# Gated scan with routed experts: the third early job in two 16-bit halves in place of plain fp32

## The chip, the core and the metric

One core of one Trainium2 chip. The metric is the device time of one execution in microseconds. Three runs of the kernel before gave 760.76, 761.78 and 762.32 us; their median, 761.78, is the time before.

## What is computed

The first half is a gated scan along the sequence, the second a mixture of experts with one expert per token (the softmax weights are cut here to what matters):

```python
f = lower + (1 - lower) / (1 + exp(-f_logit))         # (4, 3648, 256)
for t in range(S): h = f[:, t] * h + (1 - f[:, t]) * x[:, t]; y[:, t] = h
tok = y.reshape(14592, 256)
g = argmax(tok @ w_group); e = argmax(tok @ w_expert[g])   # 4 groups of 4 experts
out = g_w * e_w * (maximum(tok @ w1[g, e], 0) @ w2[g, e])  # 256 -> 1024 -> 256
```

## The kernel before, in words

The tokens are scanned in 29 units of 512 (lines 500 to 618). For a unit, its two inputs are loaded (`p1_load`, L180), ScalarE makes the gate (`p1_tanh`, `p1_affine`, L218 and L228), VectorE multiplies and scans (`p1_tb`, `p1_gate`, L244, L255, L265), TensorE transposes the result into rows and makes the routing logits (L283, L302, L315), ScalarE copies them (L285, L307, L316), and VectorE finds each token's expert and its place in that expert's list (L329 to L433; the place is `posi`, L433). GpSimd then writes the rows into the lists in DRAM with indirect DMAs, the scatters (L392). Units 0 to 7 are routed one by one, then two by two.

The experts' work is cut into jobs. Sixteen early jobs (kind "A", `EARLY`) start while the scan goes on: each takes the last rows of a list that has filled far enough by a given unit, and an expert chosen by `choose` (L648), which SP reads back as a value. Jobs 0 to 3 have 256 rows each; job 0 is cut at unit 4, job 1 at 6, jobs 2 and 3 at 8. Sixteen late jobs (kind "B") take the rest of the lists after the scan.

A job's weights come in four pieces of 128 by 1024 (`job_weights`, L933). In a split job, a piece lands in one of eight `st` buffers, which the inputs of units 4 to 7 use first; ScalarE casts it to fp16 (L949) and VectorE takes the rest in bf16 (L951). The rows are loaded (L924), transposed (L1007) and split in the same way (`xh` L1016, `xl` L1017), and the places and weights of the rows are copied aside (`meta`, L1022). The first stage (`m1_step`, L1046) takes three 16-bit products (L1063 to L1065) for each of 8 column blocks and 2 halves of K, then ScalarE's Relu (`hh`, L1068) and VectorE's remainder (`hl`, L1069), four times for 256 rows. The second stage (`m2_step`, L1080) takes three products again (L1095) for 8 blocks and each 128 rows; ScalarE scales the result (L1107), GpSimd scatters it to the output (L1109).

A job with index below `RAW` is plain ("raw"): its weights go straight into their own buffers (L937), its rows are copied (L1013) and nothing is split. The first stage (`raw1`, L1033) has one fp32 product where a split job has three, and a Relu (L1044); the second (`raw2`, L1072, L1076) likewise.

The order. SP's instructions run in the order in which the program is written. On TensorE, VectorE and ScalarE it is fixed by hand only up to the first job's preparation (L1232); after that a planner, which estimates the time of each instruction, lays down each engine's order, and the engines run that order whatever the chip's times are. `issue_after` keeps an instruction behind another in the plan: by `BEHIND` (L44, L950), a job's splits on VectorE stand behind the places of a unit; 7 is the eighth unit. The scan's work is written between the steps of the jobs (`bg_step`, L1219), at a rate that meets each job's due mark. A job's preparation (`prep_thunks`, L1174) is written while the job before it is multiplied; it also fetches further pieces of weights: up to 4 ahead for a raw job, up to 8 for a split one (L1181). A split job's second stage is written behind the next first stage, a raw job's directly behind its own:

```python
for pj, pc in ([pending] if pending else []) + ([(j, ch)] if j.raw else []):
    for t in range(len(pj.parts[pc])):
        m2_step(pj, pc, t)
pending = None if j.raw else (j, ch)
```

Of the kernel before, what the change touches and what calls it, by code (L numbers as in the profile page):

```python
# [32 lines left out]
ROWS_AT = {4: 5, 6: 7}  # L33
USED = float(1 << 22)
STG_BUFS = 8
RAW = 3
XR_BUFS = 6
ROW_BUFS = 6
O_BUFS = 5
# [1 line left out]
AHEAD = 3  # L41
STAGED = range(4, 8)
BEGIN = 6
BEHIND = {2: 7, 3: 7}  # L44
MT = -(-max(CAPS) // 128)
QUARTERS = (13, 14, 15)
ZX_SP = 12
# [5 lines left out]
def gated_scan_moe(ctx: ExitStack, tc, zx, lower, wroute, wexp, out, S):  # L53
# [28 lines left out]
    def bank(tag):  # L82
        return ps.tile([P, UNIT], F32, name=f"ps_{tag}", tag=tag, bufs=PS_BUFS[tag])
# [361 lines left out]
    def p1_thunks(us, groups, parts):  # L445
# [42 lines left out]
        def routing(v):  # L488
            grp = ends[v]
            T = sum(unit_range(x)[1] - unit_range(x)[0] for x in grp) // P  # L490
            G = {}

            def bind(G=G, first=grp[0]):
                G.update(cur.pop("G"))

            def bound(G=G, first=grp[0]):
                G["rows"] = group_rows.pop(first)
            return bind, bound, route_thunks(G, T, True)

        for u in us + [us[-1] + 1]:  # L500
            seq = []
            if u <= FAST:
# [12 lines left out]
                if ending:  # L515
                    bind, bound, (s1, f4x, s2, f3, f4, s6, f5, s7s) = routing(u - 1)
                    if u - 1 == BEHIND[2]:
                        f4.mark = "ranked"
# [302 lines left out]
    def make_job(kind, idx):  # L821
# [6 lines left out]
        while at < j.len:  # L828
# [13 lines left out]
            at += w  # L842
        j.raw = kind == "A" and idx < RAW
        j.wh, j.wl, j.st = {}, {}, {}
# [99 lines left out]
    def job_split(j, i):  # L944
# [4 lines left out]
        nc.scalar.copy(j.wh[i], j.st[i])  # L949
        with tc.issue_after(placed[BEHIND[j.idx] * 4]) if j.kind == "A" and j.idx in BEHIND else ExitStack():  # L950
            nc.vector.tensor_tensor(out=j.wl[i], in0=j.st[i], in1=j.wh[i], op=ALU.subtract)  # L951

    def job_xt(j, pi):
# [49 lines left out]
        tp = bank("p")  # L1003
        with tc.issue_after(ranked[BEHIND[2]]) if j.raw and j.idx == 1 else ExitStack():
            for k in range(KD):
# [74 lines left out]
    def m2_step(j, ch, t, pm=None):  # L1080
# [7 lines left out]
        if j.raw:  # L1088
            u = BEHIND[2] if j.idx == 0 else -1
            with tc.issue_after(ranked[u]) if u in ranked else ExitStack():  # L1090
# [238 lines left out]
```

## Time and profile before

| | |
|---|---|
| median of three runs | 761.78 us |
| the profiled execution | 760.23 us |
| its span, first to last instruction | 758.4 us |
| TensorE products (PE), busy | 718.3 us, 95% |
| TensorE weight loads (PEld), busy | 638.5 us, 84% |
| VectorE (DVE), busy | 531.1 us, 70% |
| ScalarE (ACT), busy | 450.3 us, 59% |
| GpSimd (POOL), busy | 296.0 us, 39% |

The profile is one execution on the chip. Busy time is the time in which an engine had an instruction under way; products overlap in TensorE's pipeline, so the sum of single durations is more than the busy time. In a timeline, a row gives the start, the duration, the engine, the line, the operation and its shapes; in brackets stands how long the engine was idle before, and what ended the wait. The chain is followed back from the last instruction: each step to what released it, or to the instruction before it on its engine.

### The profile page before, as it was taken

The numbers are of one execution on the slowest core, as the hardware profiler recorded it, in microseconds if no ns is written. First come the engines' busy times: TensorE is split into PE (matmuls) and PEld (weight loads), VectorE is DVE, ScalarE is ACT, GpSimd is POOL, SyncE is SP. The second block draws the span as 40 slices with busy tenths as digits, with TensorE's granted clock in tenths as the row PEclk, the third lists the DMA queues.
The fourth block names the chain that finished last, engine by engine and source line by source line (L and its number), as shares of the span: only waits on it lengthen the run. The fifth ranks groups of instructions, "written<-read, shape, count | busy, mean of one in ns | idle before, by whom it ended". The sixth has DMA issues, their size and how long they took to land.

```text
span 758.4 us, 21398 instructions
## 1 busy us (share of the span) xinstructions
PE 718.3 (95%) x8115; PEld 638.5 (84%) x8115; DVE 531.1 (70%) x1155; ACT 450.3 (59%) x824; POOL 296.0 (39%) x273
## 2 busy tenths in 40 slices
PE   3669999999999999999999999999999999999995
PEld 1557888888888888898899899999899999999995
DVE  6998779999999985687455735463754675557652
ACT  6667778876886864445454534453544465556552
POOL 3656355566855663631122212222222222223223
PEclk9969999999999999999999999999999999999998
DMA  8988899998897854567885752424354455566521
GB/s 326 397 276 278 249 378 336 382 298 294 300 315 248 251 177 149 131 178 181 187 201 155 161 129 77 133 83 122 120 143 107 142 164 139 159 177 196 172 70 35
DMA packets 101384, 152.01 MB, mean 200 GB/s; under 512 B 60898, under 2 KB 70913, under 8 KB 98464
## 3 DMA queue, kind: packets, MB, share of 16 engines
q1 hardware_dynamic: 86752, 103.27, 47.3%
q0 software_dynamic: 11408, 30.02, 10.8%
q10 hardware_dynamic: 3120, 17.34, 6.8%
q8 instruction: 64, 1.05, 0.6%
q14 instruction: 40, 0.33, 0.2%
HBM read 112.66 MB, written 38.40 MB: 199 GB/s over the span
## 4 chain that ended last, share of the span: by engine, by line
PE 62%; DVE 19%; DMA 8%; issue 4%; ACT 3%; SPq 1%; POOL 1%; POOLq 0%; ACTq 0%; DVEq 0%
PE ps_m L1095 30%; PE ps_m L1063 6%; PE ps_m L1065 6%; PE ps_m L1064 6%; DVE h L255 4%; DVE w L951 4%; PE ps_p L1063 3%; DMA st<-in_wexp_dram 3%; PE ps_p L1065 3%; PE ps_p L1064 3%; DVE hl L1069 3%; DMA xs<-rows,posi 3%; PE ps_p L283 1%; DVE zt L244 1%; ACT w L949 1%
## 5 line engine op out<-in xcount | busy, mean ns | idle before, releaser
L1095 PE MATMUL ps_m<-w,hh 128*128 128x256 bf16 (+7 forms) x2480 | 304.2, 251 | 0.0
L1095 PE MATMUL ps_m<-w,hl 128*128 128x256 f16 (+3 forms) x1240 | 250.3, 251 | 0.0
L1095 PEld LDWEIGHTS <-hh 128*128 128x128 f16 (+4 forms) x2480 | 183.1, 99 | 21.2 <-issue 2.7
L1063 PE MATMUL ps_m<-xh,w 128*128 128x256 f16 (+10 forms) x782 | 187.4, 254 | 4.7 <-DVE hl L1069 4.7
L1065 PE MATMUL ps_m<-xh,w 128*128 128x256 f16 (+10 forms) x782 | 187.2, 254 | 0.0
L1064 PE MATMUL ps_m<-xl,w 128*128 128x256 bf16 (+10 forms) x782 | 187.2, 254 | 0.0
L392 POOL DMA_INDIRECT xs<-rows,posi x114 | 141.1, 1238 | 111.3 <-ACT rows L287 25.6
L951 DVE TENSOR_TENSOR w<-st,w 128x1024 bf16<-128x1024 f32 x116 | 140.1, 1219 | 52.8 <-ACT w L949 52.5
L1109 POOL DMA_INDIRECT out_dram<-o,info x71 | 83.7, 1179 | 233.2 <-ACT o L1107 203.1
L1069 DVE SCALAR_TENSOR_TENSOR hl<-ps_m,hh 128x512 bf16<-128x512 f32 (+9 forms) x166 | 109.7, 666 | 57.2 <-ACT hh L1068 56.9
L1068 ACT ACTIVATE hh<-ps_m 128x512 f16<-128x512 f32 (+9 forms) x166 | 97.4, 588 | 65.3 <-PE ps_m L1065 64.9
L949 ACT CAST w<-st 128x1024 f16<-128x1024 f32 x116 | 120.4, 1050 | 14.1 <-PE ps_m L1095 8.1
L1064 PEld LDWEIGHTS <-w 128*128 128x128 f16 x1088 | 106.5, 98 | 12.4 <-issue 5.4
L1063 PEld LDWEIGHTS <-w 128*128 128x128 f16 x1088 | 106.5, 98 | 8.4 <-issue 1.2
L1065 PEld LDWEIGHTS <-w 128*128 128x128 bf16 x1088 | 106.4, 98 | 7.1 <-issue 0.2
L1095 PEld LDWEIGHTS <-hl 128*128 128x128 bf16 (+3 forms) x1240 | 97.7, 99 | 10.1 <-issue 0.7
L1109 POOL DMA_INDIRECT out_dram<-o,meta x51 | 59.9, 1175 | 104.8 <-ACT o L1107 93.7
L1107 ACT ACTIVATE o<-ps_m,info 128x256 f32<-128x256 f32 (+4 forms) x71 | 31.6, 445 | 73.6 <-PE ps_m L1095 65.8
L1069 DVE SCALAR_TENSOR_TENSOR hl<-ps_p,hh 128x512 bf16<-128x512 f32 (+13 forms) x65 | 41.9, 644 | 42.4 <-ACT hh L1068 42.1
L1063 PE MATMUL ps_p<-xh,w 128*128 128x256 f16 (+17 forms) x306 | 71.5, 249 | 0.0
L1064 PE MATMUL ps_p<-xl,w 128*128 128x256 bf16 (+17 forms) x306 | 71.5, 249 | 0.0
L1065 PE MATMUL ps_p<-xh,w 128*128 128x256 f16 (+17 forms) x306 | 71.5, 249 | 0.0
(179 smaller groups left out, 821.1 us busy)
## 6 DMA issues: line engine op xcount, KB each, us to landing
st<-in_wexp_dram SPq DMA_DIRECT2D x116, 512.0 KB, 7.6
zt<-in_zx_dram ACTq DMA_DIRECT2D x16, 1024.0 KB, 7.4
xs<-blank SPq DMA_DIRECT2D x28, 258.0 KB, 8.0
zt<-in_zx_dram SPq DMA_DIRECT2D x6, 1024.0 KB
w<-in_wexp_dram SPq DMA_DIRECT2D x12, 512.0 KB, 9.6
st<-in_zx_dram SPq DMA_DIRECT2D x8, 512.0 KB, 13.6
xr<-xs SPq DMA_DIRECT2D x14, 258.0 KB, 3.2
xs<-rows,posi POOLq DMA_INDIRECT x114
```

Source lines behind the costliest of these rows:

```text
L255: sn = nc.vector.tensor_tensor_scan(out=h[:, k, c0 - a:c1 - a], data0=ff[:, k, c0 - a:c1 - a], data1=uu[:, k, c0 - a:c1 - a], initial=init ...
L392: sc = nc.gpsimd.indirect_dma_start(out=xs_v[G["t0"] + t][:, :], out_offset=bass.IndirectOffsetOnAxis(ap=R["posi"][:, t:t + 1], axis=0), i ...
L949: nc.scalar.copy(j.wh[i], j.st[i])
L951: nc.vector.tensor_tensor(out=j.wl[i], in0=j.st[i], in1=j.wh[i], op=ALU.subtract)
L1063: nc.tensor.matmul(po, w1_at(j.wh, k, c), xh[:, k], start=(k == 0), stop=False)
L1064: nc.tensor.matmul(po, w1_at(j.wh, k, c), xl[:, k], start=False, stop=False)
L1065: nc.tensor.matmul(po, w1_at(j.wl, k, c), xh[:, k], start=False, stop=(k == KD - 1))
L1068: eviction[0] = nc.scalar.activation(hi, pv, AF.Relu).ins
L1069: nc.vector.scalar_tensor_tensor(out=j.hl[ch][:, cs[0]:cs[-1] + 1, 0:w], in0=pv, scalar=0.0, in1=hi, op0=ALU.max, op1=ALU.subtract)
L1095: nc.tensor.matmul(pm[i * q:i * q + n, 0:dw], h[ch][:, c, ts], w2_at(w, c)[:, i * dw:(i + 1) * dw], start=(c == 0 and s == 0), stop=(c == ...
L1107: nc.scalar.activation(o[s, 0:dw], pm[s, 0:dw], AF.Copy, scale=lt.bitcast(F32)[s, r, 1:2])
L1109: nc.gpsimd.indirect_dma_start(out=out_v[out_n[0]].rearrange("n (g d) -> (n g) d", g=g), out_offset=bass.IndirectOffsetOnAxis(ap=lt[s, r, ...
```

## The change

The constants `RAW` and `BEHIND` are changed, and nothing else. Job 2 is no longer raw: it takes the code of the split jobs, with its splits on VectorE behind the eighth unit's places. Jobs 0 and 1 stay raw. Job 3's splits are no longer kept behind these places. `BEHIND[2]`, which three other lines use for the eighth unit, keeps its value.

```diff
-RAW = 3
+RAW = 2
...
-BEHIND = {2: 7, 3: 7}
+BEHIND = {2: 7}
```

## Rows read from the trace of the kernel before

**Rows 1.** Busy us (count) by stretch: PE, PEld, DVE, ACT, POOL; clock, DMA share, GB/s.

```profile
80.00:130.00 50.00, 49.45 (x394) 41.08 (x394) 39.43 (x89) 39.54 (x77) 23.57 (x20) 1.00 0.96 327
130.00:270.00 140.00, 134.87 (x1430) 118.13 (x1428) 137.35 (x300) 110.46 (x210) 89.68 (x69) 1.00 0.87 293
270.00:720.00 450.00, 449.75 (x5345) 409.81 (x5343) 271.56 (x538) 233.84 (x402) 126.23 (x113) 1.00 0.56 149
```

**Rows 2.** The chain that ended last, 130 to 270 us, its shares by line.

```profile
by line: DVE w L951 15.3%; DVE h L255 13.2%; DVE hl L1069 11.8%; issue 7.4%; PE ps_m L1095 7.4%; DMA st<-in_wexp_dram 6.9%; DVE zt L244 5.3%; DMA xs<-rows,posi 4.4%; DVE xl L1017 3.8%; ACT w L949 2.7%; PE ps_m L1063 2.0%; PE ps_m L1065 1.6%
```

**Rows 3.** Timeline of TensorE, the third job's first products.

```profile
99.09 0.59 PE L1041 MATMUL ps_m<-xh,w 128*128 128x256 f32 x2
```

**Rows 4.** Pieces of the chain that ended last: start, us, what.

```profile
76.32 2.59 PE ps_m L1076 x12
79.35 1.73 PE ps_m L1041 x8
...
282.81 5.24 PE ps_m L1095 x48
```

**Rows 5.** Lines by source, whole span: count, then ns min/median/max.

```profile
L951 DVE TENSOR_TENSOR w<-st,w x116: 1184/1220/1227, 101.7 to 739.9; 128x1024 bf16<-128x1024 f32 x116
L1017 DVE TENSOR_TENSOR xl<-ps_p,xh x21: 415/678/692, 111.3 to 305.2; 128x512 bf16<-128x512 f32 x15, 128x256 bf16<-128x256 f32 x6
L1022 DVE COPY meta<-xr x21: 152/157/365, 111.9 to 305.8; 128x4 int32<-128x4 int32 x15, 128x2 int32<-128x2 int32 x6
L1069 DVE SCALAR_TENSOR_TENSOR hl<-ps_m,hh x166: 425/682/693, 120.4 to 743.3; 128x512 bf16<-128x512 f32 x139, 128x480 bf16<-128x480 f32 x3, 128x440 bf16<-128x440 f32 x2, 128x416 bf16<-128x416 f32 x2
L949 ACT CAST w<-st x116: 1032/1045/1117, 100.6 to 738.8; 128x1024 f16<-128x1024 f32 x116
L1016 ACT CAST xh<-ps_p x21: 364/586/684, 110.1 to 304.1; 128x512 f16<-128x512 f32 x15, 128x256 f16<-128x256 f32 x6
L1013 ACT COPY xh<-ps_p x3: 355/367/373, 57.2 to 88.0; 128x256 f32<-128x256 f32 x3
```

**Rows 6.** Timeline of VectorE, 80 to 102 us: the four longest waits.

```profile
83.96 0.32 DVE L329 TENSOR_REDUCE mx<-Lg 128x40 f32<-128x160 f32 x1 [3.31 <-ACT Lg L316]
...
92.70 1.23 DVE L244 SCALAR_TENSOR_TENSOR zt<-zt 128x1024 f32<-128x1024 f32 x1 [1.20 <-ACT zt L228]
...
96.52 0.32 DVE L329 TENSOR_REDUCE mx<-Lg 128x40 f32<-128x160 f32 x1 [1.27 <-ACT Lg L316]
...
101.67 1.23 DVE L951 TENSOR_TENSOR w<-st,w 128x1024 bf16<-128x1024 f32 x1 [2.03 <-ACT w L949]
```

**Rows 7.** SP's timeline, and the landing times of the plain jobs' weights.

```profile
64.75 2.09 SPq L937 DMA_DIRECT2D w<-in_wexp_dram  x4
...
DMA to landing us min/median/max: 8.9/9.6/13.4
```

**Rows 8.** Timeline of ScalarE, its longest waits from 76 to 100 us.

```profile
80.29 0.47 ACT L1107 ACTIVATE o<-ps_m,xr 128x256 f32<-128x256 f32 x1 [3.14 <-DMA w<-in_wexp_dram]
...
99.29 0.47 ACT L1107 ACTIVATE o<-ps_m,xr 128x256 f32<-128x256 f32 x1 [2.80 <-PE ps_m L1076]
```

**Rows 9.** Timeline of VectorE, the eighth unit's places.

```profile
68.88 0.22 DVE L433 TENSOR_REDUCE posi<-sc 128x4 int32<-128x64 f32 x1
```

**Rows 10.** A scatter's landing in the chain that ended last.

```profile
109.52 7.04 DMA xs<-rows,posi
```

**Rows 11.** Timeline of VectorE and GpSimd, a split and the scatter beside it.

```profile
104.82 1.20 DVE L951 TENSOR_TENSOR w<-st,w 128x1024 bf16<-128x1024 f32 x1
...
105.24 1.63 POOL L392 DMA_INDIRECT xs<-rows,posi  x1 [4.23 <-ACT rs L307]
...
107.17 0.97 POOL L392 DMA_INDIRECT xs<-rows,posi  x1 [0.30 <-issue]
```

**Rows 12.** Timeline of VectorE, the end of job 3's splits and its xl.

```profile
107.80 2.33 DVE L951 TENSOR_TENSOR w<-st,w 128x1024 bf16<-128x1024 f32 x2
...
111.34 0.66 DVE L1017 TENSOR_TENSOR xl<-ps_p,xh 128x512 bf16<-128x512 f32 x1
```

## The prediction

> **What bounds the kernel now.** I read the busy time by stretch first, because the shares of the whole span average over stages with different limits. Three stretches matter. From 80 to 130 us TensorE is busy 49.45 of 50 us, while VectorE has 10.57 us idle and ScalarE 10.46. From 130 to 270 TensorE (134.87 of 140) and VectorE (137.35) are both nearly full, VectorE a little more: 98.1%. From 270 to 720 TensorE alone is full [rows 1]. Then I read the chain that ended last. Between 130 and 270 its largest lines are VectorE's: the weight splits of L951, the scans of L255, the halves of L1069; TensorE's L1095 has 7.4% of it [rows 2]. So the scan stage ends when VectorE is through, and behind it TensorE runs without a gap to the end. A shift of VectorE's work before 270 us reaches the end nearly whole; a saving of TensorE before 130 us reaches it only if VectorE also gets there sooner.
>
> The edit lies where these regimes meet: the third job (index 2) starts its first stage at 99.09 us [rows 3].
>
> **Part 1, TensorE.** A plain fp32 product appears as two instructions: 12 of them stand 2.59 us in the chain, 8 stand 1.73 us, so 0.216 us for one and 0.432 for a product. Three 16-bit products cost 5.24/48 = 0.109 each, 0.327 in place of 0.432 [rows 4]. The job has 16 first-stage products (8 column blocks by 2 halves of K) and 16 second-stage ones (2 parts by 8). Removed: 32 x 0.432 = 13.8 us; added: 96 x 0.109 = 10.5. TensorE saves **3.3 us**.
>
> **Part 2, VectorE.** Added: four splits of 1.220, one xl of 0.678, one meta copy of 0.157, four hl of 0.682 [rows 5]: 4.88 + 0.68 + 0.16 + 2.73 = **8.45 us**. Nothing is taken off it. Its cover is the idle time of 80 to 130 us, of which four waits are large: 3.31 (until 83.96), 1.20, 1.27 and 2.03 (until 101.67) [rows 6]. The first three, 5.78 us, lie ahead of the job's first product, and the splits with xl and meta (5.72) would have to use them. Two splits fit into the 3.31; the next two fill 1.20 and 1.27; xl and meta, 0.84, find nothing. The four hl come after 101 us, when the gap of 2.03 is nearly over; I give them 0.6 of it and 1.0 of the small gaps behind, so 1.1 of 2.73 is uncovered. Uncovered in all: 0.84 + 1.1, about **2.0 us**. Bounds: everything covered gives 0, nothing covered 8.45. I take the value near the low end, because the large gaps and the work are of about one size.
>
> **Part 3, ScalarE.** Added: four casts of 1.045 and one xh cast of 0.586; removed: two copies of 0.367 [rows 5]. Net +4.0 us; the four Relu evictions per job stay. The weights are issued from 64.75 on and land 8.9 to 13.4 us later [rows 7], so between 74 and 80; ScalarE waits 3.14 us until 80.29 and 2.80 until 99.29 [rows 8]. These two gaps, 5.94 us, are the cover, and I price the casts at nothing. If the first gap is lost, because the casts stand in program order ahead of a landing, scans and logits behind them are late: up to 13.4 - 9.6 = 3.8 us, an end of the range.
>
> **Part 4, the holds.** The job's VectorE splits are placed behind the eighth unit's places. That unit's positions are done at 69.1 us [rows 9], the weights land after 74, so the hold costs no time; it only keeps the planner from putting a split earlier in VectorE's order. Job 3's hold goes: its splits now wait for their casts anyway (2.03 until 101.67 [rows 6]), so zero, unless the planner moves one ahead of a scan; then one such wait, 2.03 us, is the price above, and the gain below is at most the same.
>
> **Part 5, queues and buffers.** SP's four loads of the job keep their place (piece order is unchanged) but go into `st` buffers, those of units 4 and 5, freed long before 64.75: zero. Job 4 then takes job 2's buffers instead of those of units 6 and 7, so its loads wait for job 2's splits, and, since a split job prefetches further, three of these loads stand on SP ahead of the later choice of a job. If the splits are done by 97 us this hides behind job 3's four casts; if not, what is late is job 4's weights and, through SP, the next rows. The chain there runs through a scatter's landing, 7.04 us from 109.52 on [rows 10], and the row load behind it; SP is free again by then, so zero, and at worst one split, 1.22. POOL: the job's two output scatters lose their wait behind the list scatters; they reach nobody else before the end.
>
> **Part 6, the scatters.** A POOL scatter takes 0.97 us alone; the one at 105.24 met a split that ran from 104.82 to 106.02 and took 1.63 [rows 11]: 0.66 us later. The added splits lie where the lists' scatters are issued, and the chain passes through one of these at 109.52 [rows 10]. I count zero, since the added splits are done before that one, and 0.66 in the range.
>
> [...]
>
> **Sum.** TensorE's 3.3 us lie ahead of a stretch that VectorE sets, so they turn into idle time: counted 0. VectorE's uncovered work: +2.0. The profiled execution took 760.23 us (span 758.4 and 1.83 around it), so 762.2 for such a one; that execution stands 1.55 below the median of 761.78, so the median goes to **763.8**. A measurement of this kernel can tell about 0.2%, 1.5 us, from no change, so this is just on the slower side.
>
> **Rivals.**
> Faster, TensorE sets the pace: in 80 to 130 it is the full engine [rows 1], and the gaps of VectorE there end with ScalarE, which waited on TensorE. If the gaps take all 8.45 us and the stage behind starts as much earlier as TensorE does, the 3.3 us arrive whole: 761.78 - 3.3 = **758.5**. Against it: the chain of 130 to 270 is VectorE's. Chance 0.25.
>
> No difference: VectorE fills 80 to 130 as well as it fills 130 to 270, 98.1%, leaving 0.95 us idle, so up to 9.6 of the 10.57 are used; 8.45 - 9.6 = -1.2 at best, about 0 with one gap missed: 760.6 to 763.3. Chance 0.27.
>
> Clearly slower, a wait on TensorE's in-order queue: a plain job's second stage directly follows its first, while a split job's is issued behind the next job's first stage. If the planner puts job 3's first products ahead of job 2's second stage, TensorE stands from about 107 (99.1 and some 8 us for 5.2 us of products among the scan stage's) until job 3's last split (110.1) and its xl (112.0) [rows 12] with 5.2 us of ready work queued behind. That is 3 to 5 us on top of the 2.0: **767 to 769**. It decides only if nothing of the scan stage fills the hole. Chance 0.12. The forecast itself (+1.5 to +4) has 0.36.
>
> That the change doesn't do what it says can only be so for the hold, which binds nothing in time (part 4).
>
> **The numbers.** Slower: 0.36 + 0.12 = 0.48; within 0.2%: 0.27; faster: 0.25. The range runs from the faster rival, 758.5, to the wait rival with its upper price, 768.5; each side leaves out under a tenth. The forecast's own range is 763.3 to 766.
>
> **What would show it.** Right: TensorE's busy time to 130 us falls by about 3 us and its idle time between 130 and 270 rises from 5.1 towards 8 us; VectorE's gaps of 3.31, 1.20 and 1.27 are filled with L951; its idle time between 80 and 130 falls below 4 us; the last scan ends about 2 us later. Wrong: the scan stage ends earlier than before (TensorE set the pace), or a new wait of TensorE on hl, xl or L951 between 105 and 115 (the queue rival), or a new ScalarE wait on the weights' landing before 80 us.

## The result and the profile after

The changed kernel takes **771.29 us** (median of six runs, 767.36 to 772.42), the kernel before 762.25 in six runs beside it: a ratio of **1.0105** (95% interval 1.0087 to 1.0124). The direction was forecast, the size was not: +2.0 us were predicted, about four times that came, and 771.29 lies above the range. The profiled execution of the changed kernel took 772.17 us (span 770.4), 11.9 more than that of before; the median shift is 9.0, and 1.05% of 762 is 8.0. Rows of one execution are read below with that in mind.

First the busy line of the page and the first two stretches of [rows 1] in the changed kernel (PE, PEld, DVE, ACT, POOL; granted clock, DMA share, GB/s).

```profile
PE 721.4 (94%) x8147; PEld 640.1 (83%) x8147; DVE 537.9 (70%) x1165; ACT 453.9 (59%) x827; POOL 294.5 (38%) x273
```

```profile
80.00:130.00 50.00, 43.36 (x343) 33.68 (x342) 38.74 (x83) 33.74 (x65) 18.89 (x16) 0.93 0.84 278
130.00:270.00 140.00, 136.00 (x1443) 120.56 (x1441) 138.53 (x303) 113.55 (x214) 88.56 (x69) 0.99 0.91 302
```

The loss arises between 80 and 130 us: TensorE is busy 43.36 us instead of 49.45, at a mean granted clock of 0.93 instead of 1.00, and ScalarE does 5.8 us less there although it was given more to do. VectorE, which got 8.45 us of new work, is idle for 11.26 us instead of 10.57. All three wait for something. From 130 to 270 TensorE runs a little fuller than before (136.00 against 134.87). The lower clock of this stretch belongs to this execution: in another one of the same kernel (`a_again2` below, as slow against its kernel before) the clock stays at 1.00 there, and TensorE is busy even less:

```profile
80.00:130.00 50.00, 41.47 (x353) 32.96 (x352) 39.90 (x85) 35.04 (x67) 20.15 (x16) 1.00 0.83 283
```

The chain that ended last shows the same from its other side. Between 130 and 270 us its largest lines are now TensorE's, where [rows 2] had VectorE's:

```profile
by line: PE ps_m L1095 30.0%; PE ps_m L1063 10.9%; PE ps_m L1064 10.4%; PE ps_m L1065 10.3%; PE ps_p L283 6.4%; DMA zt<-in_zx_dram 5.3%; PE ps_p L302 3.7%; DVE w L951 3.5%; DVE h L255 3.5%; issue 3.1%; PE ps_p L1007 2.9%; ACT w L949 2.4%; D
```

TensorE's holes before 140 us have become work that it must catch up, with nothing left to hide them.

**Where it waits.** ScalarE's timeline around the job, in the changed kernel (start, duration, engine, line, operation, tiles; in brackets the idle time before it and what released it):

```profile
84.28 0.33 ACTq L204 DMA_DIRECT2D zt<-in_zx_dram  x1
84.67 0.60 ACT L1044 ACTIVATE hh<-ps_m 128x512 f32<-128x512 f32 x1 [4.59 <-DMA xr<-xs]
...
97.28 0.34 ACTq L204 DMA_DIRECT2D zt<-in_zx_dram  x1
97.66 1.06 ACT L218 ACTIVATE zt<-zt 128x1024 f32<-128x1024 f32 x1 [4.31 <-DMA xs<-blank]
...
107.31 1.06 ACT L218 ACTIVATE zt<-zt 128x1024 f32<-128x1024 f32 x1 [4.55 <-DMA zt<-in_zx_dram]
```

The same two transfers in the kernel before, on the same engine:

```profile
79.85 0.33 ACTq L204 DMA_DIRECT2D zt<-in_zx_dram  x1
...
87.16 0.33 ACTq L204 DMA_DIRECT2D zt<-in_zx_dram  x1
```

How to read it: an eviction from PSUM (L1044) has no use for a row load (`xr<-xs`), and a gate (L218) none for blank rows. The releaser fits the instruction ahead of each, L204: the input loads of units 13 and 14, which ScalarE issues on its own queue. The load waits, and everything behind it on ScalarE stands too: the next instruction starts 0.4 us after the load in both rows. The loads are issued 4.4 and 10.1 us later than before, and the second lands so late that the gate of its unit waits for it (4.55).

Why a load of new input waits for row loads is in the program. As it is compiled, the transfers of SP and ScalarE share eight completion semaphores (`DMAHW0` to `DMAHW7`) in turn, in planned order, and a transfer is made to wait until the earlier one on its semaphore has landed; after the change ScalarE stood 4.59 and 4.31 us at such waits. What units 13's and 14's loads wait for, by the listing of ScalarE's instructions (place, line, transfer, waits):

```
before  111 L204 DMA zt<-in_zx_dram 128x2048 [waits DMAHW7_49,DVE_49]
        127 L204 DMA zt<-in_zx_dram 128x2048 [waits DMAHW5_49]
after   115 L204 DMA zt<-in_zx_dram 128x2048 [waits DMAHW3_49,DVE_49]
        134 L204 DMA zt<-in_zx_dram 128x2048 [waits DMAHW1_49]
```

`DMAHW` names a completion semaphore, `DVE` VectorE's. Before, these were the job's last weight piece, which ended a wait of ScalarE at 79.85 too, and a row load of the next job, issued some 3 us earlier, that had landed when ScalarE came to its load at 87.16. After, they are the job's own first row load, issued at 82.11 behind scatters, and a store of blank rows, issued at 90.12. The change moved no input load; it made the third job a split one, which puts two casts ahead of the load on ScalarE and lets two more weight pieces go ahead of the blank rows on SP, and so dealt the semaphores differently.

What follows from the standing engine, on VectorE, on TensorE and on SP, in the changed kernel:

```profile
87.01 0.32 DVE L329 TENSOR_REDUCE mx<-Lg 128x40 f32<-128x160 f32 x1 [3.98 <-ACT Lg L316]
```

```profile
108.91 0.86 PE L1095 MATMUL ps_m<-w,hh 128*128 128x256 f16 x4 [1.96 <-ACT hh L1068]
...
121.37 0.65 PE L302 MATMUL ps_p<-h,wr 128*32 128x128 f32 x16 [2.37 <-DVE xl L1017]
...
135.99 0.22 PE L1063 MATMUL ps_m<-xh,w 128*128 128x128 f16 x1 [3.14 <-DVE hl L1069]
```

```profile
124.76 3.05 SPq L924 DMA_DIRECT2D xr<-xs  x4
```

The logits and the counts that ScalarE hands on (Lg, and runoff, for which VectorE waits 2.38 us until 98.81) are late, so VectorE's choice of rows is late, so the scatters and the next row loads (of the jobs with index 4 and 5) are: 124.76 us, where the kernel before has

```profile
116.74 3.10 SPq L924 DMA_DIRECT2D xr<-xs  x4
```

These 8.0 us are the size of the loss, but the two need not be equal: in `b_both` below the same loss stands beside row loads that are only 3.7 us later than before (120.41). The question for the runs was whether the input loads explain all of it.

### The profile page after: what moved, and what is told of

Its sections match the earlier page's. It is cut to its first block, busy times and chain, and to the rows that moved or that the text cites. A ratio compares the mean times of both kernels' runs of the same rounds, so it can differ in the third digit from the quotient of the medians.

```text
span 770.4 us, 21471 instructions
## 1 busy us (share of the span) xinstructions
PE 721.4 (94%) x8147; PEld 640.1 (83%) x8147; DVE 537.9 (70%) x1165; ACT 453.9 (59%) x827; POOL 294.5 (38%) x273
## 3 DMA queue, kind: packets, MB, share of 16 engines
q8 instruction: 64, 1.05, 0.5%
## 4 chain that ended last, share of the span: by engine, by line
PE 69%; DVE 12%; DMA 7%; issue 4%; ACT 3%; SPq 2%; POOL 1%; POOLq 0%; ACTq 0%; DVEq 0%
PE ps_m L1095 32%; PE ps_m L1063 8%; PE ps_m L1064 8%; PE ps_m L1065 8%; PE ps_p L1063 3%; PE ps_p L1064 3%; PE ps_p L1065 3%; DVE h L255 3%; PE ps_p L283 2%; DVE w L951 2%; DMA st<-in_wexp_dram 2%; DMA xs<-blank 2%; DMA zt<-in_zx_dram 2%; DVE hl L1069 1%; PE ps_p L302 1%
## 5 line engine op out<-in xcount | busy, mean ns | idle before, releaser
L1095 PE MATMUL ps_m<-w,hh 128*128 128x256 f16 (+3 forms) x2512 | 309.3, 251 | 3.3 <-ACT hh L1068 2.0
L1095 PE MATMUL ps_m<-w,hl 128*128 128x256 f16 (+3 forms) x1256 | 254.6, 251 | 0.2
L1095 PEld LDWEIGHTS <-hh 128*128 128x128 f16 (+3 forms) x2512 | 186.7, 99 | 25.0 <-issue 4.0
L1063 PE MATMUL ps_m<-xh,w 128*128 128x256 f16 (+12 forms) x798 | 194.1, 257 | 6.0 <-DVE hl L1069 6.0
L1064 PE MATMUL ps_m<-xl,w 128*128 128x256 bf16 (+12 forms) x798 | 194.3, 257 | 0.5 <-DVE xl L1017 0.5
L1065 PE MATMUL ps_m<-xh,w 128*128 128x256 f16 (+12 forms) x798 | 194.4, 257 | 0.0
L951 DVE TENSOR_TENSOR w<-st,w 128x1024 bf16<-128x1024 f32 x120 | 144.8, 1218 | 48.3 <-ACT w L949 48.2
L1069 DVE SCALAR_TENSOR_TENSOR hl<-ps_m,hh 128x512 bf16<-128x512 f32 (+10 forms) x170 | 112.5, 667 | 62.2 <-ACT hh L1068 61.9
L1068 ACT ACTIVATE hh<-ps_m 128x512 f16<-128x512 f32 (+10 forms) x170 | 99.5, 586 | 73.5 <-PE ps_m L1065 72.3
L949 ACT CAST w<-st 128x1024 f16<-128x1024 f32 x120 | 124.2, 1047 | 13.6 <-PE ps_m L1095 8.7
L1064 PEld LDWEIGHTS <-w 128*128 128x128 f16 x1104 | 109.0, 99 | 11.5 <-issue 3.7
L1063 PEld LDWEIGHTS <-w 128*128 128x128 f16 x1104 | 108.9, 99 | 10.0 <-issue 2.2
```

The costliest lines, as they stand in the source:

```text
L1063: nc.tensor.matmul(po, w1_at(j.wh, k, c), xh[:, k], start=(k == 0), stop=False)
L1064: nc.tensor.matmul(po, w1_at(j.wh, k, c), xl[:, k], start=False, stop=False)
L1065: nc.tensor.matmul(po, w1_at(j.wl, k, c), xh[:, k], start=False, stop=(k == KD - 1))
L1068: eviction[0] = nc.scalar.activation(hi, pv, AF.Relu).ins
L1069: nc.vector.scalar_tensor_tensor(out=j.hl[ch][:, cs[0]:cs[-1] + 1, 0:w], in0=pv, scalar=0.0, in1=hi, op0=ALU.max, op1=ALU.subtract)
L1095: nc.tensor.matmul(pm[i * q:i * q + n, 0:dw], h[ch][:, c, ts], w2_at(w, c)[:, i * dw:(i + 1) * dw], start=(c == 0 and s == 0), stop=(c == ...
```

## Experiments

Three theories. **W**: the input loads of units 13 and 14 wait for another transfer's semaphore and ScalarE stands behind them. **D**: the work added to VectorE (and ScalarE) is not covered. **S**: the 3.3 us that TensorE saves turn into a wait, because what TensorE needs next is not there earlier, and the wait costs more than it saved. (The first expectations also weigh **Q**, the order of TensorE's queue.) The chips differed (the kernel before took 778.87, 783.92, 761.73 and 759.59 us on the four, and 760.16 when the third was used again), so every ratio is to runs of the kernel before on the same chip and in the same series.

### First chip: take the waits out, put them in, add only work

`a_prefetch4`, the changed kernel with the third job prefetching only as far as a plain job does:

```diff
-            fetch_to(max(at + 1, min(at + (4 if j.raw else STG_BUFS), pptr[0] + 2)))
+            fetch_to(max(at + 1, min(at + (4 if j.kind == "A" and j.idx <= 2 else STG_BUFS), pptr[0] + 2)))
```

> The changed kernel, except that job 2 fetches weights ahead as a plain job does (up to 4 pieces, not 8), so that no piece of job 3 stands on SP between job 2's rows and the blank rows. Nothing is left out. Theory W (ScalarE stands twice because its loads of units 13 and 14 wait for the landing of job 2's row load and of a blank-row store): these two loads now share a semaphore with DMAs that have landed, ScalarE's stalls of 4.6 and 4.3 us go, and the time is 760 to 764. Theory D (VectorE's 8.45 us of added work find no cover): the work is all still there, 769 to 772. Theory Q (TensorE's queue order is what costs): the same order of stages, 769 to 772.

Measured: 1.0073 (1.0043 to 1.0103).

`b_waits`, the kernel before, whose loads of units 13 and 14 are made to wait for the same two transfers as after, besides what they wait for anyway:

```diff
+LATE_ON = {13: "rows", 14: "blank"}
...
+            if u in LATE_ON and held_by.get(LATE_ON[u]) is not None:
+                tc.add_manual_dep(last_load[u].ins, held_by[LATE_ON[u]].name, ...)
...
+                held_by["blank"] = bl.ins
...
+                    if j.idx == 2 and q == 0:
+                        held_by["rows"] = ld.ins
```

> The kernel before, with two waits added and no work: ScalarE's load of unit 13 waits for the landing of job 2's first row load, its load of unit 14 for the landing of the first of the two blank-row stores that follow. Nothing is left out. W: the same two stalls as in the changed kernel, 768 to 772. D and Q: no work and no stage moved, 761 to 763.

Measured: 1.0049 (1.0009 to 1.0089).

`b_dve` and `b_dveact`, the kernel before with four in-place operations of a split's length on the job's weights, the second with four ScalarE copies as well:

```diff
+            j.whole[i] = w
...
         if j.raw:
+            if j.idx == 2:
+                w = j.whole[i]
+                nc.scalar.copy(w, w)
+                with tc.issue_after(placed[BEHIND[2] * 4]):
+                    nc.vector.tensor_tensor(out=w, in0=w, in1=w, op=ALU.max)
```

(the line with the copy stands in `b_dveact` alone)

> The kernel before, with four VectorE instructions of a split's shape and length added on job 2's plain weights (the maximum of a weight piece with itself, which leaves it unchanged), between landing and products: 4 x 1.2 us of VectorE work and its place in the chain, without casts, without a moved load. W: 761 to 764. D: most of 4.9 us is uncovered, 765 to 767. Q: 761 to 763.

Measured: 1.0034 (0.9997 to 1.0070).

> As the run before, with a ScalarE copy of each piece onto itself ahead of each VectorE instruction, so that ScalarE's load of unit 13 is behind two of them as in the changed kernel; its semaphore is here shared with a blank-row store of 68 us. W: no long stall, 762 to 765. D: 766 to 769, ScalarE's 4.2 us on top. Q: 761 to 763.

Measured: 1.0030 (1.0002 to 1.0057).

W looks like a cause, but not the only one: taking the stalls out leaves a loss, and putting them in makes only a part of the 1.05% (the changed kernel itself did not run on this chip; the fourth chip has all three side by side). The added work by itself costs 0.3% or so; the interval of `b_dve` reaches nothing, that of `b_dveact` stays just above it. Part of the 0.34% of `b_dve` can itself be a late load: unit 13's waits for VectorE there and goes out at 82.50.

### Second chip: the hold, and VectorE's work taken off

`a_again` is the changed kernel unaltered, the yardstick on this chip.

> The changed kernel itself, so that the runs beside it have it on the same chip. All theories: 1.0% slower than the kernel before, as measured; on the chip of the last runs, where the kernel before took 779, 787.

Measured: 1.0092 (1.0059 to 1.0126).

`b_nohold3`, the second line of the change alone:

```diff
-BEHIND = {2: 7, 3: 7}
+BEHIND = {2: 7}
```

> The kernel before with the second line of the change alone: job 3's splits no longer kept behind the eighth unit's places. The planner lays down the same instructions in the same order on all engines, so every theory expects no difference: within 0.3%.

Measured: 0.9983 (0.9952 to 1.0014), no difference. Its instructions are those of the kernel before on all five engines, in the same order, so this part of the change does nothing.

`a_prefetch4_2` repeats `a_prefetch4`; `a_p4_nodve` also leaves out the job's four splits and four remainders on VectorE:

```diff
         nc.scalar.copy(j.wh[i], j.st[i])
+        if (j.kind, j.idx) == ("A", 2):
+            j.wl[i] = w[:, 0:512].bitcast(BF16)
+            return
...
+        if (j.kind, j.idx) == ("A", 2):
+            j.hl[ch] = j.hh[ch]
+            return
```

> The changed kernel with a plain job's prefetch, as in the run a_prefetch4, now beside the changed kernel. W (in part, after the first runs): 0.3 to 0.5% faster than the changed kernel, because ScalarE's two long waits go; the rest of the loss stays. If the prefetch is worth nothing: equal to the changed kernel, 1.0% slower than before.

Measured: 1.0047 (1.0014 to 1.0079).

> As the run beside it with a plain job's prefetch, but job 2 leaves out its four splits and four remainders on VectorE (7.6 us): the first half stands in for the second in all products, which stay as many. D (what is left of the loss is VectorE's work): the loss goes, and TensorE's 3.3 us may show, 0.5% faster than before to equal. If the loss is in the casts, the stages' order or the prefetch instead: 0.5 to 0.8% slower than before, as with VectorE's work.

Measured: 1.0062 (1.0037 to 1.0086).

With 7.6 us of VectorE's work gone the kernel is not faster, so **D falls** as the main cause of what W leaves; by the two intervals a part of up to some 0.3% could still be VectorE's. TensorE's waits in `a_p4_nodve` show why there is little to gain:

```profile
125.94 0.48 PE L1010 MATMUL ps_p<-ident,xr 128*128 128x128 f32 x2 [2.26 <-DMA xr<-xs]
...
134.42 0.22 PE L1066 MATMUL ps_m<-xh,w 128*128 128x128 f16 x1 [3.09 <-DVE hl L1075]
```

TensorE stands until the rows of the job with index 4 have landed, and then for VectorE's halves (hl), as it does with VectorE's work in place (2.37, 2.02 and 3.09 us in `a_prefetch4_3`, the same kernel as `a_prefetch4`, below).

### Third chip: TensorE's part alone

`b_lesspe`, the kernel before with half of the job's second stage left out (that part of its product is missing); nothing else of the change is in it, and it takes 3.46 us off TensorE, close to the 3.3 of the change:

```diff
+        if j.idx == 2:
+            cs = range(KF // 2)
         for c in cs:
             nc.tensor.matmul(pm[0:n, 0:D], j.hh[ch][c // 4][:, c % 4, c0:c0 + n],
...
-                             start=(c == 0), stop=(c == KF - 1))
+                             start=(c == 0), stop=(c == cs[-1]))
```

> The kernel before, but job 2's second stage leaves out four of its eight blocks: TensorE has 3.46 us less to do there, and nothing else is touched. Theory P (TensorE's saving is worth its length, and the loss comes from what was added): 3.4 us faster, 0.4%. Theory S (TensorE has nothing to go on with, because job 3 and 4 are supplied later, so it stands, and its granted clock falls): no faster, 0 to 0.5% slower.

Measured: **1.0029** (1.0011 to 1.0047). Less work for the engine that is 99% busy makes the kernel slower. Its TensorE timeline says how:

```profile
119.29 0.27 PE L1064 MATMUL ps_m<-xl,w 128*128 128x256 bf16 x1
119.40 0.27 PE L1065 MATMUL ps_m<-xh,w 128*128 128x256 f16 x1
123.37 0.67 PE L1007 MATMUL ps_p<-ident,xr 128*128 128x128 f32 x2 [3.70 <-DMA xr<-xs]
123.83 0.42 PE L1063 MATMUL ps_m<-xh,w 128*128 128x256 f16 x1
124.05 0.42 PE L1064 MATMUL ps_m<-xl,w 128*128 128x256 bf16 x1
...
127.25 0.63 PE L1097 MATMUL ps_m<-w,hh 128*128 128x256 f16 x2
```

its windows (columns as in [rows 1]),

```profile
120.00:124.00 4.00, 0.63 (x3) 0.58 (x4) 3.72 (x10) 4.00 (x7) 1.40 (x2) 0.78 0.99 332
124.00:128.00 4.00, 4.00 (x21) 3.02 (x19) 4.00 (x5) 2.41 (x6) 1.15 (x1) 0.50 0.95 373
128.00:132.00 4.00, 4.00 (x45) 3.06 (x44) 1.58 (x5) 0.54 (x3) 0.00 (x0) 0.87 0.64 158
```

and SP's, with the loads of the rows that TensorE then waits for (those of the job with index 4):

```profile
117.74 3.10 SPq L924 DMA_DIRECT2D xr<-xs  x4
```

The same six transposes (L1007) and what follows twelve products later, in the kernel before:

```profile
122.44 0.88 PE L1007 MATMUL ps_p<-ident,xr 128*128 128x128 f32 x6
...
124.46 0.38 PE L1095 MATMUL ps_m<-w,hh 128*128 128x256 f16 x2
```

These rows come no sooner than before, so the 3.46 us are returned as one wait of 3.70. In this execution they even come 0.9 us later (123.37 against 122.44): their loads go out 1.0 us later, and already the first cast of the fourth job's weights waits for its landing until 101.44, where it ran at 100.61 before, with SP's transfers in the same order. Behind the wait the products start some 0.215 us apart (123.83, 124.05), where before it they were 0.11 apart: the granted clock is 0.50 for all of 124 to 128 us. The six transposes and twelve products take 3.88 us (123.37 to 127.25) instead of 2.02 (122.44 to 124.46). So of the 2.8 us by which TensorE is behind at 127.25, 1.9 came with the lower clock and 0.9 with the later rows. In the kernel before it stands for no more than half a microsecond at a time there and the clock is 1.00. The ratio is worth 2.2 us, so in this execution the slow clock behind the wait is nearly as large as the loss; that it is the cause was not tried by a run that holds the clock. What lowered the clock was not shown. The length of the wait alone does not tell: `a_warm` below has one of 3.64 us with the clock at 1.00 and products 0.11 us apart behind it (123.95, 124.06).

`a_p4_peonly`, on top of the edit of `a_prefetch4`, has TensorE's part of the change and leaves out the weights' casts and splits and the remainders; xh, xl and meta stay (the upper bf16 half of the fp32 weights stands in for both halves):

```diff
+        if (j.kind, j.idx) == ("A", 2):
+            j.wh[i] = j.wl[i] = j.st[i].bitcast(BF16).rearrange("p (n two) -> p n two", two=2)[:, :, 1]
+            return
...
+        if (j.kind, j.idx) == ("A", 2):
+            j.hl[ch] = j.hh[ch]
+            return
```

> The changed kernel with a plain job's prefetch, but job 2 leaves out its casts, splits and remainders: the upper half of each fp32 weight stands in for both halves, so that of the change only TensorE's part is left (16-bit products, second stage behind job 3's first), with xh, xl and meta. P: 3 us faster than before. S: equal to before or up to 0.5% slower.

Measured: 1.0043 (1.0024 to 1.0062). The wait is there again, and longer, and the clock from 124 to 128 us is 0.50 again:

```profile
126.47 0.70 PE L1010 MATMUL ps_p<-ident,xr 128*128 128x128 f32 x2 [7.42 <-DMA xr<-xs]
```

`a_p4_noact`, on top of the same edit, leaves out only the casts (the same view as above stands in for the high half):

```diff
-        nc.scalar.copy(j.wh[i], j.st[i])
+        if (j.kind, j.idx) == ("A", 2):
+            j.wh[i] = j.st[i].bitcast(BF16).rearrange("p (n two) -> p n two", two=2)[:, :, 1]
+        else:
+            nc.scalar.copy(j.wh[i], j.st[i])
```

> As the run before it, but with the splits and remainders on VectorE back in; only the four casts on ScalarE are left out. Theory A (the casts stand in ScalarE's chain of the scan between 77 and 91 us and push it back): like the run before it, and 0.3 to 0.6% faster than the changed kernel with a plain job's prefetch. D: 0.4 to 0.6% slower than the run before it.

Measured: 1.0150 (1.0134 to 1.0166), a miss, and a fault of the experiment rather than of the casts. VectorE's timeline:

```profile
70.08 1.23 DVE L954 TENSOR_TENSOR w<-st 128x1024 bf16<-128x1024 f32 x1 [1.33 <-DMA st<-in_wexp_dram]
72.92 1.22 DVE L954 TENSOR_TENSOR w<-st 128x1024 bf16<-128x1024 f32 x1 [1.61 <-DMA st<-in_wexp_dram]
...
76.52 1.23 DVE L954 TENSOR_TENSOR w<-st 128x1024 bf16<-128x1024 f32 x1 [1.99 <-DMA st<-in_wexp_dram]
...
80.58 1.23 DVE L954 TENSOR_TENSOR w<-st 128x1024 bf16<-128x1024 f32 x1 [1.11 <-DMA st<-in_wexp_dram]
```

Without a cast ahead of it, each split is laid in VectorE's order before its piece has landed, and VectorE stands 6.0 us in all with scans queued behind. Unit 13's load, which also waits for VectorE, goes out at 84.21 instead of 81.04 (`a_prefetch4_3`), and ScalarE stands 7.89 us until 84.68 behind it. So nothing on the casts' own price follows, but something on order: a step that waits for a landing must not stand ahead of the scan.

`a_warm` tries to hold the clock, on a guess of the author's that work in a wait does so: `a_prefetch4` with 24 idle products ahead of the transposes and of the first products of jobs 3 and 4.

```diff
+        if j.kind == "A" and j.idx in (3, 4) and pi == 0:
+            keep_warm(bank("m2"), 24)
...
+        if j.kind == "A" and j.idx in (3, 4) and ch == 0 and cs[0] == 0:
+            keep_warm(bank("m2"), 24)
```

> The changed kernel with a plain job's prefetch, and 24 short products on constants ahead of the row transposes and of the first products of jobs 3 and 4 (96 in all, about 5 us of TensorE's work at the higher clock), which fill a part of its waits. S, as far as the clock goes: the granted clock stays at 1.00 between 105 and 140 us, and the time is 0.2 to 0.4% under that of the same kernel without them. If the clock has no part: 0 to 5 us slower than that.

Measured: 1.0091 (1.0074 to 1.0107), no gain. The clock was 1.00 from 80 to 130 us (third number from the end):

```profile
80.00:130.00 50.00, 44.98 (x436) 38.16 (x435) 43.06 (x92) 38.56 (x74) 19.78 (x17) 1.00 0.86 301
```

But so it was in `a_prefetch4_3`, the same kernel without idle products, so they did not win this:

```profile
80.00:130.00 50.00, 41.22 (x363) 33.98 (x363) 43.09 (x92) 38.91 (x74) 21.47 (x18) 1.00 0.89 313
```

Where the clock fell there (0.66 from 132 to 136 us) it fell here too, a little less and later (0.84 from 136 to 140). On TensorE's timeline the idle products (L292) and the wait are apart:

```profile
104.06 1.50 PE L292 MATMUL ps_m<-upto,tri 128*128 128x128 bf16 x24
106.71 1.11 PE L292 MATMUL ps_m<-upto,tri 128*128 128x128 bf16 x17
108.69 1.89 PE L292 MATMUL ps_m<-upto,tri 128*128 128x128 bf16 x31
...
123.53 0.48 PE L1009 MATMUL ps_p<-ident,xr 128*128 128x128 f32 x2 [3.64 <-DMA xr<-xs]
```

Three groups ran between 104 and 111 us, 4.5 us in all, ahead of products that were ready; the wait for the rows still came at 120 (3.64 us). So they are work added to a queue that had some, and the wait itself was not filled. `a_prefetch4` did not run on this chip, so what they cost is not known. What a held clock is worth was not tried by this run and stays open.

### Fourth chip: both causes together, and W from both sides

`b_both` is the kernel before with the edits of `b_waits` and `b_lesspe`; the other three are repeats in more runs.

> The kernel before with both suspected costs put in and nothing else of the change: the loads of units 13 and 14 wait on ScalarE's queue for job 2's first row load and for a blank store, and job 2's second stage leaves out four of its eight blocks (3.46 us less for TensorE; that part of job 2's product is missing). Theory W+S (the two causes are separate and together they are the loss): 1.0075 to 1.011, about the sum of the run with the waits alone (1.0049) and the run with less TensorE work alone (1.0029), and as slow as the changed kernel within 0.2%. W alone (TensorE's part costs nothing of its own): 1.005 or less. If VectorE's and ScalarE's added work is a third cause: clearly under the changed kernel, by 0.3% or more.

> The changed kernel itself beside the other three on the same chip. 1.0085 to 1.0125 if this chip is like the ones before.

> The changed kernel with the third job prefetching as far as a plain one, so that the loads of units 13 and 14 meet other semaphores. W: 0.3% to 0.5% under the changed kernel on the same chip, and the rest (S and what VectorE adds) stays, 1.004 to 1.007. If ScalarE's stalls are not a cause: within 0.15% of the changed kernel.

> The kernel before with the two waits of ScalarE's loads put in by hand. W: 1.003 to 1.006, about what the changed kernel loses over the one that prefetches as before. If the stalls are harmless: within 0.15% of 1.

| kernel | us | ratio to before | interval |
|---|---|---|---|
| `a_again2`, the change | 768.65 | 1.0107 | 1.0088 to 1.0127 |
| `b_both`, before with W and S | 767.50 | **1.0107** | 1.0090 to 1.0124 |
| `b_waits2`, before with W | 765.43 | 1.0074 | 1.0055 to 1.0093 |
| `a_prefetch4_3`, the change without W | 764.42 | 1.0058 | 1.0042 to 1.0073 |

`b_both` holds none of the change's casts, splits, remainders or 16-bit products, and is as slow as the change. **W and S together are enough for a loss of this size**, and no third cause is needed for it. That they are the same shares in the change is not shown: the waits put in by hand are not those of the change (in `b_both` the loads go out at 83.00 and 92.28, in the change at 84.28 and 97.28), and the ones taken out are not all gone (81.04 and 91.11 in `a_prefetch4_3`, 79.85 and 87.16 before). W is worth 4.2 us taken out (768.65 - 764.42; the intervals of the two ratios do not touch) and 5.8 put in (765.43 - 759.59); S alone was 0.29% on the third chip, 2.2 us, and 0.74% + 0.29% = 1.03% meets the 1.07% measured. With the 0.49% that the first chip gave for W put in, the sum would be 0.78%. From the other side, 0.49% for W taken out leaves 0.58%, so how the loss divides is known only roughly: W 0.49 to 0.74%, the rest 0.29 to 0.58%, in which up to 0.3% of added work can hide. TensorE's wait in `b_both`, with both causes, is longer than in `b_lesspe` (timeline, then windows):

```profile
128.40 0.67 PE L1016 MATMUL ps_p<-ident,xr 128*128 128x128 f32 x2 [5.75 <-DMA xr<-xs]
```

```profile
124.00:128.00 4.00, 0.00 (x0) 0.00 (x0) 3.72 (x10) 4.00 (x7) 1.25 (x2) 0.83 1.00 378
128.00:132.00 4.00, 3.60 (x17) 2.90 (x18) 3.83 (x7) 1.00 (x3) 1.26 (x1) 0.50 0.76 294
```

In `b_waits2`, with nothing but the waits added, ScalarE stands behind the loads and VectorE waits 6.22 us where [rows 6] had 3.31:

```profile
83.17 0.47 ACT L1116 ACTIVATE o<-ps_m,xr 128x256 f32<-128x256 f32 x1 [6.53 <-DMA xr<-xs]
```

```profile
86.36 0.32 DVE L334 TENSOR_REDUCE mx<-Lg 128x40 f32<-128x160 f32 x1 [6.22 <-ACT Lg L321]
```

In `a_prefetch4_3` the same loads go out at 81.04 and 91.11 (84.28 and 97.28 in the change), and no wait for rows or blanks is left on ScalarE (a wait of 2.38 us, now put down to TensorE, stays in front of its work at 81.46):

```profile
81.04 0.37 ACTq L204 DMA_DIRECT2D zt<-in_zx_dram  x1
91.11 0.34 ACTq L204 DMA_DIRECT2D zt<-in_zx_dram  x1
...
101.95 1.06 ACT L218 ACTIVATE zt<-zt 128x1024 f32<-128x1024 f32 x1 [2.54 <-DMA zt<-in_zx_dram]
```

The next row loads go out at 118.67 there: 6.1 of their 8.0 us are won back, for 4.2 us of time. What stays is TensorE, which stands for them all the same, and for VectorE's halves:

```profile
116.01 0.64 PE L302 MATMUL ps_p<-h,wr 128*32 128x128 f32 x16 [2.37 <-DVE xl L1017]
...
121.73 0.48 PE L1007 MATMUL ps_p<-ident,xr 128*128 128x128 f32 x2 [2.02 <-DMA xr<-xs]
...
130.19 0.22 PE L1063 MATMUL ps_m<-xh,w 128*128 128x128 f16 x1 [3.09 <-DVE hl L1069]
```

### Third chip again: the loads on SP's queue

If a standing ScalarE is the harm, another queue should cure it, and the kernel before should gain too: its wait of 3.14 us until 80.29 [rows 8] ends with unit 13's load, issued at 79.85.

`a_zxsp15` (from the change) and `b_zxsp14` (from before):

```diff
-ZX_SP = 12
+ZX_SP = 15
```

```diff
-ZX_SP = 12
+ZX_SP = 14
```

> The changed kernel with the input loads of units 12, 13 and 14 issued on SP's queue instead of ScalarE's. If ScalarE standing in its own queue is what costs (W): the waits of 4.6 and 4.3 us in front of ScalarE's work until 85 and 98 us are gone, and the ratio to before falls from 1.0107 by 0.3 to 0.6%, to 1.005 to 1.008; a rest of up to 0.3% stays if SP issues unit 14's load as late as ScalarE did. If it is the late landing alone that costs: within 0.2% of the changed kernel, since SP's queue has the same waits.

> The kernel before with the input loads of units 12 and 13 on SP's queue. It tries the reading that the 3.14 us wait of ScalarE until 80.29 in the kernel before is unit 13's load waiting in ScalarE's queue, and not work of ScalarE that wants the weights. If so, that wait is gone and the time is 0.995 to 1.000 of before; if unit 13's load on SP comes too late behind the blank rows (after 85 us instead of 79.85), the gain is lost, 1.000 to 1.005. If the wait stays at its place, the reading is wrong.

Measured: 1.0132 (1.0109 to 1.0156) and 1.0128 (1.0095 to 1.0161). Both expectations of a gain failed, and `b_zxsp14` lost more than the 1.000 to 1.005 that it was given for a late load. SP's and ScalarE's timelines in `a_zxsp15`:

```profile
84.30 0.41 SPq L204 DMA_DIRECT2D zt<-in_zx_dram  x1
```

```profile
90.82 1.06 ACT L218 ACTIVATE zt<-zt 128x1024 f32<-128x1024 f32 x1 [8.60 <-DMA zt<-in_zx_dram]
```

and in `b_zxsp14`:

```profile
81.09 0.37 SPq L204 DMA_DIRECT2D zt<-in_zx_dram  x1
```

```profile
87.20 1.06 ACT L218 ACTIVATE zt<-zt 128x1024 f32<-128x1024 f32 x1 [5.97 <-DMA zt<-in_zx_dram]
```

The old waits are gone: in `b_zxsp14` nothing on ScalarE waits for weights near 80 us any more, as the reading of [rows 8] said. The output eviction behind that wait does not come much sooner, though: it now waits 2.72 us until 78.47 for TensorE. SP, however, issues unit 12's load only behind its row loads, at 84.30 and 81.09 us instead of 69 on ScalarE, and the gate waits for the landing, 8.60 and 5.97 us. So **a late landing of the input** costs as well, with those loads gone from ScalarE's queue; standing in ScalarE's queue is one way to be late, standing in SP's another, and here a worse one. How much of W is the standing engine and how much the late input these two runs do not part, because they also made unit 12's load late. No version that was run beats the kernel before.

## Why the prediction missed

**Part 5 is the step that failed.** It followed SP's four loads and the `st` buffers and ended at "zero, and at worst one split, 1.22". It never looked at the other queue, ScalarE's own input loads (L204), which the change does not touch: two casts now stand ahead of unit 13's load, two weight pieces go before the blank rows on SP, and with the new order the loads wait for other transfers. Measured: 4.2 to 5.8 us on the fourth chip. Part 5 also had "SP is free again by then, so zero" for the next row loads; they came 8.0 us later. The sign was in [rows 8], which part 3 read as cover: the 3.14 us until 80.29 stand before an output eviction and end with a landing of weights. An eviction of `ps_m` needs no weights in `w`; the transfer in front of it did. What was taken for free time to hide casts in was the very wait that the change made longer.

**Part 1** had the saving right in kind and mis-sized in effect. "They turn into idle time: counted 0" is half of it. They did turn into idle time, 3.70 us for 3.46 in `b_lesspe`, but the kernel with that idle time was 2.2 us slower; in the profiled execution 1.9 us went with the lower clock behind it. The text listed the clock beside [rows 1] (1.00 in every stretch) and did not ask what would become of it once TensorE had a hole. Over the span of the changed kernel's profile TensorE's busy time rose from 718.3 to 721.4 us although about 3.3 us of work went; in `a_again2` it fell to 716.9, by less than half of that.

**Part 2**, priced at +2.0, is not what was measured. The splits ran at 78.33 and 90.02 us in pairs, partly in the gaps that were meant for them, but the gaps were longer than forecast. Adding the work costs 0.34% with an interval from -0.03 to 0.70, taking it off gains nothing (1.0062 against 1.0047), and `b_both` needs none of it. The runs' best values for it lie between 0 and 0.34%; they do not tell it from zero.

**Part 3**: the casts' own price stays untested, since `a_p4_noact` made waits of its own. `b_dveact`, with copies of their length ahead of the same load, lost no more than `b_dve`, which points to the transfer waited for, and not to the casts in front, as what makes W. **Part 4** is right: the hold changes no instruction. **Part 6**: zero fits. The scatters' time on GpSimd from 60 to 140 us, before and then after (busy, count, clock):

```profile
60.00:140.00 80.00, 31.05 (x26) 1.00 0.93 316
```

```profile
60.00:140.00 80.00, 29.82 (x24) 0.94 0.84 275
```

that is 1.19 and 1.24 us for one. The mean grew by 0.05 us. It is no test of splits against none: L951 runs 12 times in these 80 us in both kernels (14.32 us before, 14.11 after); four of the 12 after are the job's own (78.33 and 90.02).

**The rivals.** The faster one is refuted directly: taking TensorE's work off, alone, costs 0.29%. The sum's premise, that VectorE sets the pace from 130 to 270 us, did not outlast the change: the largest lines of that chain are TensorE's now. The queue rival gave 767 to 769 us and the low end of the measured spread (767.36) lies there, but by another mechanism. The wait of TensorE until 108.91 is not for splits behind a planner's choice; it is for hh, which ScalarE evicted right behind its gate of 107.31, and that gate had waited 4.55 us for unit 14's load. Of the signs named ahead, a new wait of TensorE between 105 and 115 us did come (1.96), but on hh and not on hl, xl or L951. "Its idle time between 80 and 130 falls below 4 us" failed (11.26), TensorE's busy time to 130 us fell by 6.5 instead of 3, its idle time from 130 to 270 fell to 4.0 instead of rising towards 8, and the last scan starts 7.4 us later (272.1 against 264.7), not 2.

## What to carry to other kernels

When a change adds or moves transfers or work on an engine that also issues loads, list for each load of that queue which earlier transfer it waits for, before and after; a long wait in front of an instruction that has no use for its releaser belonged here to a transfer ahead of it (3.14 us before, 4.59 and 4.31 after), and was no free time. Ask of work taken from a full engine whether what feeds it comes sooner; here, on TensorE, 3.46 us less of it made the kernel 0.29% slower (`b_lesspe`).

## What the runs showed of the hardware

Taking 3.46 us of products off TensorE made the kernel 0.29% slower (1.0011 to 1.0047): one wait of 3.70 us, then products 0.215 us apart instead of 0.11 for some 5 us. That a shared completion semaphore held an unrelated input load for more than 4 us, and the issuing engine with it, was not expected either (4.59 and 4.31 us). Other partners on the shared semaphores were worth 4.2 us (`a_prefetch4_3` against `a_again2`, 764.42 against 768.65).
